# Side work put in front of a block until its tokens are there, and one function table for ScalarE

## The chip, the cores and the metric

The kernel runs on one core of a Trainium2 chip. Its engines each run their own instructions in the order in which the program wrote them, and wait for each other by semaphores: PE (TensorE, matmuls), DVE (VectorE), ACT (ScalarE), POOL (GpSimd) and SP (SyncE, which here only issues DMAs). The metric is device time in microseconds (us) for one launch; smaller is better.

## What is computed

7168 tokens of 192 numbers pass three stages: a causal convolution over 7 tokens whose weights are a softmax of their own for each token and head, then a mixture of 8 experts of which each token takes its best two, then a second mixture of which each token takes one.

```python
w = softmax(weight_gen)                                # attention: 7 taps, 8 heads
out = einsum('bshk,bskhg->bshg', w, windows_of(x))
# first mixture, top 2 of noisy logits
noisy = x @ w_gate + log1p(exp(x @ w_noise)) * noise
for e in range(8):                                     # tokens whose top 2 hold e
    out[mask] += top2_w * (relu(x[mask] @ w1[e]) @ w2[e])   # 192 -> 1024 -> 192
# second mixture, top 1 of softmax(x @ w_gate)
for e in range(8):
    out[mask] = gate * (relu(x[mask] @ w1[e]) @ w2[e])
```

## The kernel before

The work has **five phases**. Phases 0, 1 and 2 are the first mixture, each for a group of tokens; phases 3 and 4 are the second. Within a phase the tokens are sorted by expert into blocks of 128, and one or two blocks of an expert make a **unit**. A phase can begin once it is routed: the logits of its tokens, the choice of experts, and the lists `src` (which token stands where) and `dest` (where its result goes) are there.

A unit runs as follows. POOL gathers each block's token rows with an indirect DMA (`gt<-rows,src`, `load_x`), SP transposes them by DMA (`xt<-gt`, `turn_x`), PE multiplies with the first weights (L1, `ph<-xt,wres`; numbers in fp32 are carried as pairs of fp16, so that 5 matmuls make 128 of the 1024 hidden values), ACT makes the high half of the rectified result (`hh<-ph`) and DVE the low half (`hl<-ph,hh`), PE multiplies with the second weights (L2, `py<-wres,hh` and `py<-wres,hl`), ACT copies the sum out (`yo<-py`, two buffers), and POOL scatters it (`ybuf<-yo,dest` in phases 0 to 2, `out_dram<-yo,dest` later). A unit of one block has two L1 steps of 20 matmuls (128x128) and 24 L2 matmuls, a unit of two blocks four steps of 10 (128x256) and 48.

The main loop over units writes the L1 steps of unit i alternating with the L2 steps of unit i-1 (`l1_step` at 1487, `l1_late`, `l2_step`, loop at the end of the kernel). Gathers are issued up to three units ahead (`prepare`), but only of phases that are routed. Where the next unit belongs to a phase that isn't routed yet, the loop first writes all L2 steps of the last unit and then everything that the routing still needs (`feed.until(lambda: ph.ready)`), and only then the gathers and the L1 of that unit.

Everything else is **side work**: the convolution and its taps (`acc`, `tmp`, `xs`, `wg`), splitting the experts' weights into fp16 halves (`wres`, `wacc`, `wsc`, `wbt`; small matmuls `pm<-wacc,onesf` add up a scale), logits, the routing of the next phase (`lg`, `ra`, `rb`, `rc`, `rd`; `pr<-msk,..`, `pr<-bex,pex`, `pr<-rb,lost`, then `src`, `segt`, `ge`, `pr<-ge,ones`, `be`, `dest`), and combining results. It is written as threads of steps, and a planner decides at build time where each step stands. The planner (`Clock`, 77) keeps a modelled time for every engine and buffer from fixed costs. `Feed.pump` (257) is called after each L1 step and each L2 step: it takes steps, as long as there are any whose inputs the model has ready by the time at which PE is free (`clk.free["P"]`), with a small allowance for each engine, and writes them there. `clk.ready(a)` is the modelled time at which a buffer is written. On the chip nothing of that model remains; only the order does.

All recorded instructions of the helper carry its line, L189, so rows are told apart by names. ACT's functions come in tables, and the compiler writes a table load (ACT_TABLE_LOAD) in front of a function whose table isn't the loaded one. Exp, Ln, Relu, Abs, Copy and Square are used.

Of the kernel before, what the change touches and what calls it, by code (L numbers as in the profile page):

```python
# [16 lines left out]
P = 128  # L17
# [193 lines left out]
class Feed:  # L211
# [42 lines left out]
                best = (t + th[2], th)  # L254
        return best and best[1]

    def pump(self):
        while True:
            th = self.pick(self.clk.free["P"])
            if th is None:  # L260
                return
            self.step(th)
# [9 lines left out]
def moe_kernel(ctx: ExitStack, tc: tile.TileContext, x: bass.AP, wgen: bass.AP,  # L272
               g1: bass.AP, n1: bass.AP, noise: bass.AP, w11: bass.AP, w12: bass.AP,
               g2: bass.AP, w21: bass.AP, w22: bass.AP, out: bass.AP):
    nc = tc.nc
    clk = Clock()
    V, A, G, PE, SP = [Eng(e, k, clk) for e, k in (
        (nc.vector, "V"), (nc.scalar, "A"), (nc.gpsimd, "G"), (nc.tensor, "P"), (nc.sync, "S"))]
    feed = Feed(clk)

    def new_pool(name, side=None, **kw):
        if side:
            kw["side"] = side
        return Pool(tc.alloc_tile_pool(name=name, bufs=1, **kw), clk, name.startswith("ps"))
# [1063 lines left out]
    for pi, ph in enumerate(phases):  # L1348
# [6 lines left out]
        for it in dyn + [None] + stat if pi == 2 else stat + dyn + [None]:  # L1355
# [4 lines left out]
            u = Unit()  # L1360
# [126 lines left out]
    def l1_step(u, s):  # L1487
        T = u.nb * P
        fs = 512 // T
        ps = psm.tile([P, 512], F32, name="ph", bufs=4)  # L1490
        for fi in range(fs):
            f = s * fs + fi
            w = u.w1[f // 4]
            fo = (f % 4) * P
            o = ps[:, fi * T:(fi + 1) * T]
            for j, (wo, xi) in enumerate(((0, 0), (0, 2), (512, 0), (1024, 1), (1024, 3))):
                PE.matmul(o, w[:, wo + fo:wo + fo + P], u.xt[:, xi], start=(j == 0), stop=(j == 4))
        hh = blk.tile([P, 512], F16, name="hh", bufs=5)
        hl = blk.tile([P, 2 * RW], F16, name="hl", bufs=5)[:, 0:512]
        A.activation(hh, ps, AF.Relu)  # L1500
        u.h.append((hh, hl))
        late.append((ps, hh, hl))
# [98 lines left out]
    def seldom(ph):  # L1601
# [7 lines left out]
        with tc.If(used > ph.ndyn):  # L1609
            with tc.For_i(b0, used + ph.base, NR) as i:  # L1610
                us = []
                for k in range(NR):
                    u = Unit()
                    u.ph, u.nb, u.b0, u.e, u.rare, u.last = ph, 1, 0, None, True, False
                    u.ns, u.h = 2, []
                    u.src, u.dest, u.bei = [blk.tile([P, 1], I32, name=f"{v}{k}") for v in ("srcr", "destr", "beir")]
                    V.tensor_copy(u.src, ph.src[:, ds(i + k, 1)])
                    V.tensor_copy(u.dest, ph.dest[:, ds(i + k, 1)])
                    V.tensor_copy(u.bei, ph.bei[:, ds(i + (k - ph.base), 1)])
                    us.append(u)  # L1620
                for u in us:
                    load_x(u)
                for k, u in enumerate(us):
                    turn_x(u)
                    if ph.m:
                        u.gate = blk.tile([P, 1], F32, name=f"gater{k}")
                        V.tensor_tensor(u.gate, u.g[0][:, 256:257], ph.undo[:, ds(i + (k - ph.base), 1)], op=ALU.mult)
                for u in us:
                    for half, step in enumerate((l1_step, l2_step)):
                        for _ in fetch(u, half):  # L1630
                            pass
                        for k in range(u.ns):
                            step(u, k)
                            l1_late()
                    l2_out(u)
# [38 lines left out]
    for i in range(nu + 1):  # L1674
        u = units[i] if i < nu else None
# [35 lines left out]
        for k in range(n):  # L1711
            while s1 < n1 and s1 * n <= k * n1:
                l1_step(u, s1)
                s1 += 1
                if s1 == n1 and u.last:
                    passed.add((u.e, 0))
                    feed.n += 1
                feed.pump()
            l1_late()
            for _ in range(4 // n):  # L1720
                next(jobs, None)
            if TP:
                turns(i)
            while s2 < n2 and (s2 + 1) * n <= (k + 1) * n2:
                l2_step(prev, s2)
                s2 += 1
                if s2 == n2:
                    l2_out(prev)
                feed.pump()
# [39 lines left out]
```

## Time and profile before

| | before |
|---|---|
| median of 3 runs | 1016.14 us (1012.07 to 1022.45) |
| the profiled execution | 1023.41 us, its span 1021.6 us |
| mean granted TensorE clock in it | 0.945 of full speed |
| PE busy | 899.0 us, 88% of the span |
| DVE busy | 761.2 us, 75% |
| ACT busy | 511.9 us, 50% |
| POOL busy | 431.4 us, 42% |

A row of the timeline gives start, length, engine, line, operation, what is written from what, the tile, and in brackets how long the engine was idle just before and what ended that. Starts are us from the span's start. The granted clock is a share of full speed: 1.00 stands for 2.4 GHz, 0.50 for 1.2 GHz. SPq and POOLq are an engine's sequencer, which issues DMAs.

### The profile page before, as it was taken

To read this page: it belongs to the slowest core of one execution; us is meant where nothing else is said; L and a number is where in the kernel's file an instruction comes from. 1 tells how busy PE (TensorE), PEld (TensorE's weight loads), DVE (VectorE), ACT (ScalarE), POOL (GpSimd) and SP (SyncE) were. 2 spreads that over 40 slices of the span, in tenths; PEclk is the share of its full clock that TensorE was granted. 3 is DMA by queue.
4 is the path that set the end of the run, shared out by engine and by line. 5 is a ranking of instruction groups with operands and counts; after the bars stand their busy time and mean duration, and the time that the engine had idled before them with its cause. 6 is when DMAs were issued, how large, how long until landed. Compare 5 with 4: busy or idle time off the path is not lost. (4 is left out here: it accounts for less than half of the span.)

```text
span 1021.6 us, 26687 instructions
## 1 busy us (share of the span) xinstructions
PE 899.0 (88%) x10354; PEld 828.4 (81%) x10354; DVE 761.2 (75%) x1854; ACT 511.9 (50%) x1024; POOL 431.4 (42%) x575
## 2 busy tenths in 40 slices
PE   2896269999997999999679999999989998999985
PEld 0453158989996799999679988998989998999985
DVE  7587758999987798968577768988678987355442
ACT  1333147774441444546356778855666633444432
POOL 4020035555534455543443434444545443464541
PEclk8898569999998899999789999999999999999998
DMA  9257079998671678653489999856468547453692
GB/s 278 58 135 159 0 139 226 244 201 188 155 144 41 158 162 175 166 116 112 112 178 260 205 205 251 191 129 155 115 175 191 126 118 210 98 121 85 196 241 81
DMA packets 216802, 160.97 MB, mean 158 GB/s; under 512 B 147996, under 2 KB 198511, under 8 KB 216668
## 3 DMA queue, kind: packets, MB, share of 16 engines
q1 hardware_dynamic: 197932, 114.34, 46.7%
q0 software_dynamic: 18736, 44.85, 18.8%
q8 instruction: 84, 1.38, 0.6%
q14 instruction: 50, 0.41, 0.1%
HBM read 74.46 MB, written 32.59 MB: 105 GB/s over the span
## 5 line engine op out<-in xcount | busy, mean ns | idle before, releaser
L189 ACT ACTIVATE hh<-ph 128x512 f16<-128x512 f32 x362 | 214.8, 595 | 325.8 <-PE ph L189 284.3
L189 PE MATMUL ph<-xt,wres 128*128 128x256 f16 (+1 forms) x3200 | 327.1, 255 | 24.7 <-DMA xt<-gt 13.1
L189 DVE SCALAR_TENSOR_TENSOR hl<-ph,hh 128x512 f16<-128x512 f32 x362 | 245.5, 685 | 114.5 <-ACT hh L189 101.2
L189 PEld LDWEIGHTS <-wres 128*128 128x128 f16 x3200 | 265.0, 100 | 46.8 <-issue 20.3
L189 PE MATMUL py<-wres,hh 128*128 128x192 f16 x2048 | 273.9, 247 | 7.0 <-ACT yo L189 6.4
L189 PEld LDWEIGHTS <-hh 128*128 128x128 f16 x2896 | 261.0, 98 | 14.1 <-issue 9.4
L189 POOL DMA_INDIRECT gt<-rows,src x181 | 195.8, 1082 | 144.4 <-DVE wmx L189 72.6
L189 POOL DMA_INDIRECT ybuf<-yo,dest x120 | 138.5, 1154 | 271.8 <-ACT yo L189 258.6
L189 PE MATMUL py<-wres,hl 128*128 128x192 f16 x1024 | 253.0, 247 | 0.0
L189 PE MATMUL ph<-xt,w 128*128 128x128 f16 (+1 forms) x1600 | 136.8, 240 | 18.6 <-DMA xt<-gt 7.6
L189 PEld LDWEIGHTS <-hl 128*128 128x128 f16 x1448 | 142.0, 98 | 0.3 <-DVE hl L189 0.2
L189 PEld LDWEIGHTS <-w 128*128 128x128 f16 x1600 | 115.8, 100 | 26.9 <-issue 8.9
L189 POOL DMA_INDIRECT out_dram<-yo,dest x61 | 63.4, 1039 | 120.7 <-ACT yo L189 70.4
L189 PE MATMUL py<-w,hh 128*128 128x192 f16 x848 | 114.0, 248 | 0.1
L189 PE MATMUL py<-w,hl 128*128 128x192 f16 x424 | 105.0, 248 | 0.0
L189 PE MATMUL acc<-prod,identf 128*128 128x384 f32 x168 | 63.1, 535 | 14.1 <-DVE prod L189 11.7
L189 PEld LDWEIGHTS acc<-prod,identf 128*128 128x128 f32 x168 | 34.1, 208 | 36.5 <-DVE prod L189 11.7
L189 DVE COPY w<-wres 128x3072 f16 x53 | 51.0, 968 | 13.2 <-issue 5.8
L189 ACT ACTIVATE yo<-py 128x192 f32<-128x192 f32 x120 | 37.1, 327 | 38.5 <-DMA ybuf<-yo,dest 22.8
L189 DVE SCALAR_TENSOR_TENSOR wres<-w,wsc,wres 128x1024 f16<-128x1024 f32 (+1 forms) x32 | 49.4, 1545 | 4.9 <-ACT wres L189 4.9
L189 ACT ACTIVATE wres<-w,wsc 128x1024 f16<-128x1024 f32 (+1 forms) x32 | 43.5, 1359 | 12.2 <-DVE wsc L189 11.4
L189 DVE TENSOR_TENSOR acc<-acc,tmp 128x768 f32<-128x768 f32 (+1 forms) x60 | 47.9, 798 | 2.1
(206 smaller groups left out, 901.3 us busy)
## 6 DMA issues: line engine op xcount, KB each, us to landing
w<-wres SPq DMA_DIRECT2D x23, 768.0 KB
rows<-rows SPq DMA_DIRECT2D x24, 512.0 KB
w<-in_moe_w_dram SPq DMA_DIRECT2D x14, 768.0 KB
w<-in_moe_w_dram SPq DMA_DIRECT2D x13, 512.0 KB
xs<-in_x_dram SPq DMA_DIRECT2D x6, 960.0 KB
rows<-ybuf SPq DMA_DIRECT2D x10, 384.0 KB
yl<-ybuf SPq DMA_DIRECT2D x10, 384.0 KB
wres<-wbt SPq DMA_DIRECT2D x56, 64.0 KB
```

The source lines that it names most:

```text
L189: return fn(*args, **kw)
```

## The change

Three edits. `pump` may be given a time up to which side steps are taken in, later than PE's modelled free time. Before the first L1 step of each unit that isn't a rarely run one, `pump` is called with the later of the modelled times at which the unit's transposed tokens and its first weights are there; steps that can start by then are written ahead of the unit's matmuls. And one call at the kernel's start loads a table that holds both Exp and Ln.

```diff
-    def pump(self):
+    def pump(self, upto=0.0):
         while True:
-            th = self.pick(self.clk.free["P"])
+            th = self.pick(max(upto, self.clk.free["P"]))
             if th is None:
                 return
             self.step(th)
...
     feed = Feed(clk)
+    nc.scalar.preload_act_table_set("natural_log_exp_and_others")
...
     def l1_step(u, s):
         T = u.nb * P
         fs = 512 // T
+        if s == 0 and not u.rare:
+            feed.pump(max(clk.ready(a) for a in (u.xt, u.w1[0])))
         ps = psm.tile([P, 512], F32, name="ph", bufs=4)
```

The order on ACT around the first block, before. The first rc is the end of the first part of phase 0's noise, `ra` and the second `rc` belong to its second part, and the first `hh` is that of the first block:

```order
L189 ACT_TABLE_LOAD
L189 ACTIVATE rc<-rb 128x128
L189 ACTIVATE ra<-lg_128 128x64
L189 ACT_TABLE_LOAD
L189 ACTIVATE ra<-ra 128x64
L189 ACT_TABLE_LOAD
L189 ACTIVATE rc<-rb 128x64
L189 ACTIVATE hh<-ph 128x512
L189 ACT_TABLE_LOAD
L189 ACTIVATE wg_541<-wg_541 128x112
L189 ACTIVATE wres,wacc_930<-w_352 128x1536
```

The same stretch of ACT in the change:

```order
L189 ACTIVATE rc<-rb 128x128
L189 ACTIVATE ra<-lg_129 128x64
L189 ACTIVATE ra<-ra 128x64
L189 ACTIVATE rc<-rb 128x64
L189 ACTIVATE wg_542<-wg_542 128x112
L189 ACTIVATE wres,wacc_918<-w_353 128x1536
L189 ACTIVATE wres<-w_353,wsc_922 128x2x512
L189 ACTIVATE wbt_927<-w_353,wsc_922 128x512
L189 ACTIVATE hh<-ph 128x512
```

The table loads are gone, and a softmax of the convolution (`wg`) and three weight passes stand ahead of the first block's `hh`. On PE, likewise, `pr<-identf,ra` and a `pm<-wacc,onesf` now stand ahead of the first block's first matmul; in before they stood behind its first 20 and first 50.

The order on POOL at the end of phase 0, before. The first row is the scatter of a block of the unit two before the last; `spacer` is a short memset; each gather is of phase 1:

```order
L189 DMA ybuf_68<-yo,dest 9216x192
L189 MEMSET spacer 1x1
L189 DMA ybuf_68<-yo,dest 9216x192
L189 MEMSET spacer 1x1
L189 DMA ybuf_68<-yo,dest 9216x192
L189 MEMSET spacer 1x1
L189 DMA ybuf_68<-yo,dest 9216x192
L189 DMA gt<-rows_66,src 128x256 x10
L189 MEMSET spacer 1x1
```

The same place of POOL in the change, from the same scatter on:

```order
L189 DMA ybuf_69<-yo,dest 9216x192
L189 DMA gt<-rows_67,src 128x256 x6
L189 MEMSET spacer 1x1
L189 DMA ybuf_69<-yo,dest 9216x192
L189 MEMSET spacer 1x1
L189 DMA ybuf_69<-yo,dest 9216x192
L189 DMA gt<-rows_67,src 128x256 x2
L189 MEMSET spacer 1x1
L189 DMA ybuf_69<-yo,dest 9216x192
```

Six gathers of phase 1 moved ahead of the last three scatters of phase 0, and the others alternate with scatters.

The order on DVE where phase 1's list of tokens is done, before. `ISA src` is the last row that the gathers need; no `hl` (a block's low half) stands here:

```order
L189 ISA src<-rb,rc 128x176
L189 TENSOR_TENSOR segt<-segs,id_95 128x16
L189 TENSOR_REDUCE segt<-segt 128x1
L189 TENSOR_SCALAR ge<-ip,segt 16x56
L189 CAST be<-pr 128x56
L189 TENSOR_SCALAR be<-be 128x56
L189 CAST be<-segs 128x1
L189 TENSOR_SCALAR rd<-ra 128x88
```

The same place of DVE in the change:

```order
L189 ISA src<-rb,rc 128x176
L189 TENSOR_TENSOR segt<-segs,id_96 128x16
L189 TENSOR_REDUCE segt<-segt 128x1
L189 TENSOR_SCALAR ge<-ip,segt 16x56
L189 SCALAR_TENSOR_TENSOR hl<-ph,hh 128x512
L189 TENSOR_TENSOR tmp<-xs_3469,wg_3470 128x768
L189 TENSOR_TENSOR acc_4091<-acc_4091,tmp 128x768
L189 SCALAR_TENSOR_TENSOR hl<-ph,hh 128x512
L189 CAST be<-pr 128x56
```

Two `hl` of blocks still stand behind `src`: phase 1's routing is done while blocks of phase 0 run. On PE, `pr<-rb,lost` moved forward by the same way: in before it stands right ahead of phase 1's first matmul, in the change ahead of the last unit's L1.

## Rows read from the trace of the kernel before

**Rows 1.** The page, busy us (share of the span) x instructions of each engine.

```profile
PE 899.0 (88%) x10354; PEld 828.4 (81%) x10354; DVE 761.2 (75%) x1854; ACT 511.9 (50%) x1024; POOL 431.4 (42%) x575
```

**Rows 2.** Windows: stretch, length, busy by engine, granted clock, DMA share, GB/s.

```profile
100.00:150.00 50.00, 19.17 (x160) 16.13 (x159) 32.34 (x110) 10.83 (x16) 8.66 (x10) 0.55 0.27 58
150.00:200.00 50.00, 47.36 (x514) 44.22 (x512) 44.26 (x97) 40.00 (x67) 26.25 (x29) 1.00 1.02 228
...
300.00:350.00 50.00, 39.97 (x399) 35.95 (x397) 38.06 (x111) 13.97 (x26) 17.91 (x22) 0.86 0.35 82
```

**Rows 3.** Waits of PE: who waited for what, us in total, times, longest.

```profile
PE ph L189 <- DMA xt<-gt: 20.7, 4, 10.0
...
PE ph L189 <- issue: 9.5, 1, 9.5
...
PE pm L189 <- ACT wres L189: 1.6, 2, 0.8
```

**Rows 4.** Timeline of PE at the first block.

```profile
140.04 2.29 PE L189 MATMUL ph<-xt,wres 128*128 128x128 f16 x20 [9.50 <-issue]
142.26 0.65 PE L189 MATMUL pr<-identf,ra 128*39 128x128 f32 x2
...
146.43 0.28 PE L189 MATMUL pm<-wacc,onesf 128*128 128x1 f32 x2
```

**Rows 5.** Groups of ACT by line: busy us, mean ns, idle before.

```profile
L189 ACT ACT_TABLE_LOAD x11 | 14.1, 1283 | 3.0 <-DMA wres<-in_weight_gen_dram 2.8
```

**Rows 6.** Timeline of ACT in the routing of phase 0.

```profile
95.38 1.28 ACT L189 ACT_TABLE_LOAD   x1
96.67 0.31 ACT L189 ACTIVATE rc<-rb 128x128 f32<-128x128 f32 x1
...
104.89 1.28 ACT L189 ACT_TABLE_LOAD   x1
```

**Rows 7.** Timeline of DVE in the same stretch.

```profile
97.01 0.29 DVE L189 SCALAR_TENSOR_TENSOR rb<-rb,ra 128x128 f32<-128x128 f32 x1 [1.85 <-ACT rc L189]
...
104.90 0.19 DVE L189 TENSOR_SCALAR rb<-ra 128x64 f32<-128x64 f32 x1 [1.89 <-ACT ra L189]
```

**Rows 8.** Timeline of PE, phase 0 to phase 1.

```profile
312.92 1.28 PE L189 MATMUL ph<-xt,wres 128*128 128x128 f16 x20
314.04 0.33 PE L189 MATMUL py<-wres,hh 128*128 128x192 f16 x2
314.20 0.25 PE L189 MATMUL py<-wres,hl 128*128 128x192 f16 x1
...
323.94 0.45 PE L189 MATMUL pr<-rb,lost 39*128 39x88 f32 x2
334.43 2.29 PE L189 MATMUL ph<-xt,wres 128*128 128x256 f16 x10 [10.03 <-DMA xt<-gt]
```

**Rows 9.** Timeline of DVE at the same place.

```profile
325.87 0.21 DVE L189 TENSOR_SCALAR src<-ra 128x88 int32<-128x88 f32 x1
```

**Rows 10.** Timeline of POOL at the same place.

```profile
314.51 0.99 POOL L189 DMA_INDIRECT ybuf<-yo,dest  x1 [0.22 <-issue]
...
326.99 0.98 POOL L189 DMA_INDIRECT gt<-rows,src  x1 [1.10 <-DVE segt L189]
```

**Rows 11.** Windows behind two gaps, columns as in rows 2.

```profile
334.40:340.00 5.60, 5.58 (x27) 3.72 (x28) 2.95 (x10) 2.69 (x4) 2.74 (x3) 0.50 0.87 168
...
524.40:527.80 3.40, 3.40 (x30) 3.30 (x28) 3.16 (x9) 2.64 (x6) 2.01 (x3) 0.50 1.06 83
```

**Rows 12.** Timeline of PE and POOL, phase 1 to phase 2 and after.

```profile
505.68 4.42 PE L189 MATMUL ph<-xt,w 128*128 128x128 f16 x40 [7.58 <-DMA xt<-gt]
...
523.23 1.32 PE L189 MATMUL ph<-xt,w 128*128 128x128 f16 x20 [2.74 <-DVE w L189]
...
496.59 1.00 POOL L189 DMA_INDIRECT ybuf<-yo,dest  x1 [4.18 <-ACT yo L189]
497.89 0.98 POOL L189 DMA_INDIRECT gt<-rows,src  x1 [0.30 <-issue]
```

## Prediction

> **What bounds the kernel now.** I read the page's first part first: TensorE (PE) is busy 899.0 of 1021.6 us, VectorE (DVE) 75% [rows 1]. A PE at 88% leaves 122 us of gaps and of matmuls at a lower clock, so I looked for these with the table of windows. Two of the three stretches shown in [rows 2] are poor: 100 to 150 us (PE 19.17 of 50, granted clock 0.55) and 300 to 350 us (39.97, clock 0.86); at 150 to 200 us PE has 47.36 of 50 at clock 1.00. The list of waits says what PE waits for there: 9.5 us once for "issue" (the first block) and 20.7 us in four waits for the transposed tokens xt, the longest 10.0 [rows 3]. The timeline puts places to them: the first block's L1 starts at 140.04 after 9.50 us idle [rows 4]; the first block of phase 1 starts at 334.43 after 10.03 us idle [rows 8]; the first of phase 2 at 505.68 after 7.58 us [rows 12]. These are the places where a block's tokens come late, and so those where this change can act. Inside a phase PE runs without a gap and a moved step changes only the order.
>
> Each such gap costs more than itself. Behind the gap at 334 us the granted clock is 0.50 (the 1.2 GHz level) from 334.4 to 340.0 [rows 11]: 5.6 us at half speed, 2.8 us lost. Behind a gap of 2.74 us at 523.23 [rows 12] it is 0.50 for 3.4 us [rows 11]: 1.7 us lost.
>
> **Part one, the table of functions.** Before has 11 table loads of 1283 ns on ScalarE (ACT), 14.1 us together [rows 5]; the order of the change has one, ahead of everything. What a load is worth depends on who waits. Over the span ACT is half idle [rows 1], so I count the loads among the blocks at nothing: what hides them is that PE runs other matmuls until hh comes, and where that cover fails up to 1.28 us more is won for each. Three loads lie in the chain that routes phase 0, before any block can run, the first at 95.38, the last at 104.89 [rows 6]. DVE has nothing else to do then: it sits 1.85 us until rc comes at 97.01, 1.89 us until ra at 104.90 [rows 7], and again until the Ln behind the third load. Without them the chain is shorter by at most 3 x 1.283 = 3.85 us. The third load starts at 104.89 and rb takes 0.19 us of DVE from 104.90 beside it, which stays, and the logits that DVE scales after the first chain have their own time from PE; I take 3.5 us, with 2.6 (two loads) and 3.85 as ends.
>
> The row shows the Ln of the first load starting at 96.67, which is 1.29 us after the load began [rows 6]: the load costs its own length and nothing behind it. The Trainium skill, page "ScalarE: Activation LUTs", section "What ACT_TABLE_LOAD costs", states about 1283 ns for the load, as here, and about 1380 ns more for a drain, 2.66 us for each switch; by that page the three would be worth about 8 us, an estimate, and the forecast about 4.5 us lower. No run here shows that drain after a load; one that lies ahead of the load would be hidden in the idle of ACT, so I go by the rows.
>
> **Part two, the first block.** The new call stands ahead of the first matmuls of each unit. At the very first one it puts the steps that can start by then into the 9.50 us wait. On PE two rows move in front: pr<-identf,ra, 0.65 us, and pm<-wacc, 0.28 us, which in before stood behind the first 20 matmuls and more [rows 4]. That is 0.9 us less behind the wait, at the half clock too. On ACT the softmax of the conv weights and the first expert's weight passes move ahead of the first hh. On DVE conv taps and a weight pass move ahead of the first hl. If they run over the 9.50 us, PE waits for hl at its first L2: between nothing and 0.8 us, the longest wait of PE for a weight pass in before [rows 3]. So this part lies between -0.9 and -0.1; I take -0.1, since both DVE and ACT get more to do ahead of that L2, and with the table loads **the start gives -3.6 us**.
>
> **Part three, the boundary from phase 0 to phase 1.** This is the large term. In before the routing of phase 1 ends behind the last block of phase 0. PE's lost counts (pr<-rb,lost) run at 323.94, DVE writes the list src at 325.87, POOL issues the first gather at 326.99 [rows 8 to 10], and PE's next matmul is the block at 334.43 [rows 8]. From gather to L1 is 7.44 us (gather, transpose, landing). The last unit's L2 has been drained by then, since the program waits here when the phase isn't routed. All engines but POOL and SP idle.
>
> In the order of the change the routing of phase 1 stands earlier against the blocks: six gathers stand on POOL ahead of three scatters that preceded them before, and on DVE the src row has an hl of phase 0 in front and two more right behind. The first new gather follows the scatter that in before started at 314.51 and took 0.99 us [rows 10]. I set that scatter as mark: in before the unit it belongs to ended its matmuls at 312.92, where the next x20 begins [rows 8]. So with E = 312.92 the scatter ends at E + 2.6 and the gather starts at E + 2.9 (0.30 us between POOL's rows [rows 12]). src is ready by then, as its rows stand ahead of the last unit. L1 of phase 1 then comes at E + 2.9 + 7.44 = E + 10.3. What can PE do between? By the order: two L1 steps of the last unit (x20 at 1.12 us from start to start each [rows 8]), 24 and 24 matmuls of L2 at 0.08 us (two in 0.16 [rows 8]), and a few small ones of routing and gates, which I put at 0.5 to 1.0 us beside the 0.45 of the lost counts: 2.2 + 3.9 + 0.5 to 1.0 = 6.7 to 7.2 us. A gap of 3.1 to 3.6 us is left, of the size of that at 523 us, and so with 1.7 us of half clock: 5.3 us at most, against 10.03 + 2.8 = 12.8 us before. The last unit's L2 is now emitted between L1 steps of phase 1, not drained, so it fills nothing in that gap but isn't lost either. **Boundary: -7.5 us**. Ends: -5 (the transposes land two to three us later, because they now share DMA with the traffic of blocks; at the boundary to phase 2 their wait is 7.58 us) and -12.8 (whole gap hidden).
>
> What a wait more costs here: the six gathers stand on POOL in order, so the scatters behind them come up to 6 x 1.3 us later (0.98 and 0.30 for each). yo has two buffers, so ACT's copies of the last unit, and then PE's py, wait for the scatters. I leave it inside the lower end.
>
> **Part four, the rest.** The boundary to phase 2 at 505.68 is bound on POOL: the first gather at 497.89 follows a scatter at 496.59 directly, not DVE [rows 12]. The change moves the routing of phase 2 some two us later against the blocks; I count 0, and 2 us slower where DVE takes POOL's place as the last. Inside phases only orders change: 0, with 2 us either way.
>
> **Sum.** 1023.41 is the profiled run (its span 1021.6 us and 1.8 around it). -3.6 - 7.5 = -11.1 us gives 1012.3. The median of before, 1016.14, lies 7.3 us (0.7%) under this run, which is within what three runs scatter (1012.07 to 1022.45). Against the median the forecast is 1016.1 - 11.1 = **1005 us**, a ratio of 0.989. About 1% (10 us) is what a measurement of this kernel can tell from no change.
>
> **Rivals.** (a) The forecast, 0.45: 1002 to 1008.
> (b) The gap at phase 1 closes altogether and PE's clock stays at its upper level: -12.8 - 3.6 = -16.4, **1000 us**. For it: the routing stands early enough; POOL's gather need only come 3 us sooner. Against it: the scatter of the unit before stands in front of the gather. 0.2.
> (c) The start is won and the boundary hardly: transposes queue behind the DMA traffic of blocks (DMA share 1.02 at 150 to 200 us [rows 2]), or the 7.58 us gap at phase 2 grows by what phase 1 starts earlier. -3.6 and 0 to -3: **1011 us**, 0.25.
> (d) Slower. The call puts matmuls of side work in front of a block's own on a queue that runs in order, if the planner's clock says that their inputs are there first. If its clock is wrong, PE stands for them. This phase has 16 weight pieces with one small matmul each, which waits for ACT's pass over a piece. In before the worst such waits are 0.8 us (pm behind ACT wres) [rows 3] and 2.74 us (ph behind DVE's copy w) [rows 12], each rarely. Sixteen at 0.8 us make 12.8, more than the 11.1 won; it decides from 0.7 us each. At the 2.74 us row it would be 44 - 11 = 33 us slower. At 1.4 us each: 22 - 11 = +11, **1027 us**. For it: DVE has 44.26 of 50 busy and DMA 1.02 in that phase [rows 2], so the inputs do run late at times. Against it: a step goes ahead only where the modelled input is ready, and in before the same planner left no such wait above 0.8 us. 0.1. The Trainium skill, "TensorE: Matmul & The Clock Gate", section "Step-by-step: what each phase is for", speaks for this rival: matmuls stay in program order and only weight loads are pulled ahead; nothing in the rows above shows a matmul overtaking.
>
> **How the numbers follow.** The range reaches from (b), 1000 less 2 us for the rest and 1 for the table loads' upper end, to (c) with the rest at +2 to 3: **997 to 1014**; outside lie (d) and a tenth of the others. Faster by over 1% means 1006.0 or less: two thirds of (a), all of (b), little of (c): 0.52. Within 1%: the rest of (a) and (c): 0.39. Slower: most of (d), 0.09.
>
> **What would show it.** Right: one table load; the first L1 at 136 to 137 us of the span; the first gather of phase 1 directly behind the scatter of the unit before, with phase 0's last L2 still to come, and the gap ahead of its L1 at 2 to 5 us, with clock 0.50 behind it for some 3 us. Wrong: a gap there of over 7 us (c) or none (b); waits of pm or pr for ACT, DVE or DMA that add up to over 10 us in 140 to 330 us (d); DVE's hl waits ahead of the first L2; the gap ahead of phase 2 grown by more than 2 us.

## The result and the profile after

The changed kernel takes 1004.43 us (median of 14 runs, 999.61 to 1013.91) against 1018.45 us of the kernel before (14 runs beside them, 1012.07 to 1022.45): ratio **0.9872**, 95% interval 0.9848 to 0.9897, that is 14.0 us or 1.3% faster. The forecast was 1005 us, a ratio of 0.989, faster by 11.1 us. Its range held the time. Later sets of runs did not agree on the gain: in one where the kernel before takes 1065 us the whole change gave nothing, in one where it takes 1021 us it gave 18.4 us, and in one at 1057 us, which had the parts alone, these gave little. That is the subject of most of the experiments.

The page after, and PE's list of waits:

```profile
PE 893.2 (89%) x10354; PEld 826.2 (83%) x10354; DVE 763.3 (76%) x1853; ACT 500.3 (50%) x1015; POOL 429.0 (43%) x575
...
PE ph L189 <- DMA xt<-gt: 15.4, 4, 7.1
...
PE pm L189 <- ACT wres L189: 7.0, 5, 3.1
...
PE py L189 <- ACT yo L189: 1.3, 4, 0.4
```

PE is busy for 893.2 us where it was 899.0 [rows 1], with the same 10354 matmuls, at a mean granted clock of 0.955 where it was 0.945. Its longest wait for tokens is 7.1 us instead of 10.0 [rows 3]. The wait of `pm` for a weight pass on ACT grew from 1.6 to 7.0 us, of which 3.1 lie ahead of the first block, where PE has nothing else to do. The line for "issue" (9.5 us at the first block) is gone, because other rows of PE now stand in that wait. The wait is divided by them and hardly filled: 1.86, 3.14 and 3.51 us of it are left, as the rows of PE below show.

**The chain ahead of the first block**, on ACT, DVE and POOL of the changed kernel, to be held against [rows 6] and [rows 7]:

```profile
93.86 0.41 ACT L189 ACTIVATE rows<-rows 128x256 f16<-128x256 f16 x1 [0.64 <-DVE rows L189]
94.18 0.29 ACT L189 ACTIVATE rc<-rb 128x128 f32<-128x128 f32 x1
...
100.85 0.26 ACT L189 ACTIVATE ra<-lg 128x64 f32<-128x64 f32 x1 [6.38 <-DVE lg L189]
101.14 0.26 ACT L189 ACTIVATE ra<-ra 128x64 f32<-128x64 f32 x1
101.65 0.26 ACT L189 ACTIVATE rc<-rb 128x64 f32<-128x64 f32 x1 [0.26 <-DVE rb L189]
```

```profile
94.50 0.29 DVE L189 SCALAR_TENSOR_TENSOR rb<-rb,ra 128x128 f32<-128x128 f32 x1 [0.43 <-ACT rc L189]
...
101.43 0.19 DVE L189 TENSOR_SCALAR rb<-ra 128x64 f32<-128x64 f32 x1 [0.61 <-ACT ra L189]
101.94 0.23 DVE L189 SCALAR_TENSOR_TENSOR rb<-rb,ra 128x64 f32<-128x64 f32 x1 [0.32 <-ACT rc L189]
```

```profile
129.58 1.09 POOL L189 DMA_INDIRECT gt<-rows,src  x1 [69.17 <-DVE wmx L189]
```

The same two ends of the chain in before:

```profile
94.94 0.42 ACT L189 ACTIVATE rows<-rows 128x256 f16<-128x256 f16 x1 [0.64 <-DVE rows L189]
...
134.13 1.02 POOL L189 DMA_INDIRECT gt<-rows,src  x1 [72.63 <-DVE wmx L189]
```

Nothing stands between `rows` and `rc` any more, and DVE's waits of 1.85 and 1.89 us shrank to 0.43 and 0.61. From the start of the last `rows<-rows` ahead of the chain to the first gather it is 129.58 - 93.86 = 35.72 us. In before it is 134.13 - 94.94 = 39.19 us. The difference is 3.47 us. The rest of the earlier start, 1.08 us, was there before the chain began and differs between any two executions.

**The first block and the boundary to phase 1**, PE and POOL:

```profile
127.85 0.65 PE L189 MATMUL pr<-identf,ra 128*39 128x128 f32 x2 [1.86 <-DVE ra L189]
131.63 0.59 PE L189 MATMUL pm<-wacc,onesf 128*128 128x1 f32 x2 [3.14 <-ACT wres L189]
135.73 6.11 PE L189 MATMUL ph<-xt,wres 128*128 128x128 f16 x50 [3.51 <-DMA xt<-gt]
...
148.29 0.38 PE L189 MATMUL pm<-wacc,onesf 128*128 128x1 f32 x2 [1.73 <-ACT wres L189]
...
310.48 1.28 PE L189 MATMUL ph<-xt,wres 128*128 128x128 f16 x20
...
314.06 1.28 PE L189 MATMUL ph<-xt,wres 128*128 128x128 f16 x20
...
320.96 3.35 PE L189 MATMUL ph<-xt,wres 128*128 128x256 f16 x20 [3.64 <-DMA xt<-gt]
```

```profile
312.12 1.01 POOL L189 DMA_INDIRECT ybuf<-yo,dest  x1 [0.22 <-issue]
313.44 0.98 POOL L189 DMA_INDIRECT gt<-rows,src  x1 [0.30 <-DVE acc L189]
```

```profile
320.96:324.00 3.04, 3.04 (x20) 2.39 (x21) 2.94 (x4) 0.60 (x1) 2.61 (x5) 0.69 1.22 124
324.00:327.00 3.00, 3.00 (x26) 2.74 (x25) 2.90 (x4) 0.60 (x1) 2.69 (x2) 0.75 0.72 153
327.00:330.00 3.00, 3.00 (x33) 2.79 (x31) 2.96 (x5) 1.53 (x3) 1.25 (x4) 1.00 0.29 87
```

The windows have the columns of [rows 2]. PE starts phase 1 after a gap of 3.64 us, where it was 10.03 [rows 8]. The first gather stands directly behind the scatter, as the order had it, 0.30 us after its end, and 7.52 us ahead of the L1. Behind the gap the clock is 0.69 and 0.75 in two windows of 3 us and then 1.00: (0.31 x 3.04) + (0.25 x 3.00) = 1.7 us lost.

### The profile page after: what moved, and what is told of

It reads as the page before. It is cut to its first block, busy times and chain, and to the rows that moved or that the text cites. A ratio compares the mean times of both kernels' runs of the same rounds, so it can differ in the third digit from the quotient of the medians.

```text
span 999.2 us, 26672 instructions
## 1 busy us (share of the span) xinstructions
PE 893.2 (89%) x10354; PEld 826.2 (83%) x10354; DVE 763.3 (76%) x1853; ACT 500.3 (50%) x1015; POOL 429.0 (43%) x575
## 5 line engine op out<-in xcount | busy, mean ns | idle before, releaser
L189 POOL DMA_INDIRECT gt<-rows,src x181 | 199.1, 1100 | 136.3 <-DVE wmx L189 69.2
L189 POOL DMA_INDIRECT ybuf<-yo,dest x120 | 133.7, 1115 | 263.0 <-ACT yo L189 241.2
```

Source lines behind the costliest of these rows:

```text
L189: return fn(*args, **kw)
```

## Experiments

Each was run beside the kernel before in the same set, and its ratio is to that; e6 and e12 are single runs, made for their traces. The record names the chip of each of these sets: number 3 for e1 to e8, where the kernel before takes 1057 and 1065 us, and number 7 for e9 to e12, where it takes 1021 us. For the first set it names none.

### The two parts apart: e1 and e2

e1 keeps only the table load, e2 only the call.

```diff
 e1:
-        if s == 0 and not u.rare:
+        if s == 0 and False:
 e2:
-    nc.scalar.preload_act_table_set("natural_log_exp_and_others")
```

> The table of functions loaded once, and nothing else of the change: the new call ahead of a unit's first L1 step is left out. By the forecast only the three loads in the chain that routes phase 0 count: 3.5 us less, ratio 0.9966, the first gather about 3.5 us earlier against the first rc of that chain (beginning of rc to first gather 37.5 us in before, 35.4 after the change with one load ahead of the rc gone too), the gap ahead of phase 1 at 10 us as in before. By the rule of 2.66 us for each switch some 8 us would come off before the first gather, ratio 0.992. If the loads inside the phases delay PE as well, up to 14 us, ratio 0.986.

> The call ahead of a unit's first L1 step alone, with the 11 table loads of before. By the forecast the boundary to phase 1 gives 7.5 us and the start next to nothing: 1011 against 1018.45, ratio 0.992 to 0.993, gap ahead of phase 1 at 3 to 4 us. If the later phases gain from the order too, as the two traces seem to say (some 7 us between 511 and 839 us), ratio 0.986 or less. If the two parts need each other, ratio over 0.996.

The kernel before took 1057.4 us in this set. e1 gave a ratio of 0.9974 (0.9944 to 1.0004), within its interval the forecast's 0.9966 and neither 0.992 nor 0.986. Its gap ahead of phase 1 is 10.33 us, as expected. e2 gave **1.0064** (1.0038 to 1.0090): the call alone made the kernel slower here, against every expectation of a gain. So either the boundary's gain wasn't one, or something in this set took it back.

### The call by phases: e3 and e4

e3 calls `pump` only for units of phase 0, e4 only for those of the later phases; both keep the table.

```diff
 e3:
-        if s == 0 and not u.rare:
+        if s == 0 and not u.rare and u.pi == 0:
 e4:
+        if s == 0 and not u.rare and u.pi >= 1:
```

> The table and the call, but the call only for units of phase 0. By the forecast this is the whole of the change: 1004 to 1007, ratio 0.987 to 0.989, gap ahead of phase 1 at 3 to 4 us. If the later phases gain by the call (rival), ratio 0.992 to 0.995, since some 7 us are missing.

> The table and the call, but the call only for units of phases 1 to 4. By the forecast this gives the table's 3.5 us and no more: ratio 0.9965, with 2 us either way, gap ahead of phase 1 at 10 us as in before. If the later phases gain by the call (rival), ratio 0.988 to 0.992.

e3 gave 0.9971 (0.9939 to 1.0004), e4 0.9936 (0.9910 to 0.9962), in the same set as e1 and e2. Neither tells the theories apart: the call that should win all wins nothing over the table alone (e1, 0.9974), and the one that should win nothing wins some. In e4 the gap ahead of phase 1 is 7.09 us, too, and not the 10 us expected.

### Again, with the kernel before traced beside it: e5 to e8

In e3 the gathers of phase 1 started early, as in the changed kernel (322.30 us), but PE's first L1 of that phase came 11.75 us behind the first one instead of 7.5. The next set therefore held the whole change (e5), the kernel before (e6, for its trace), a version that puts the gathers ahead of the scatters (e7), and e3 again (e8).

```diff
 e7, at the end of a unit's L2:
                 if s2 == n2:
+                    nxt = todo["load"]
+                    if u is not None and nxt < nu and nxt > i and units[nxt].pi != u.pi and units[nxt].ph.ready:
+                        prepare(min(i + 1, nxt), False)
                     l2_out(prev)
```

> The whole change once more. In the four runs so far (the kernel before at 1057 us there) the boundary's gain showed only in part: between the first gathers of phase 1 and its first L1, PE got its instructions one or two at a time, about 0.7 us apart, though it waited for nothing that the trace shows. Theory 1: that is where these runs were made, and not the change; then the whole change gives 0.9872 again where the kernel before takes about 1018 us, and 0.995 to 1.0 where it takes 1057 us, with the same stall of 5 to 8 us ahead of phase 1. Theory 2: the earlier result was a lucky order; then the ratio is over 0.993 anywhere.

> The kernel before, for its trace beside the others of this set. Theory 1: where the set runs at 1057 us, the share of PE's idle time that nothing visible ends is as large here as in the changed kernels, but in the 10 us wait ahead of phase 1 it costs nothing; where the set runs at 1018 us there is next to none of it. Theory 2: there is none of it in the kernel before in either case.

> The whole change, and one thing more: when the next gathers are the first of a new phase that is routed, they are issued ahead of the scatters of the unit before and not behind them. After the change the first gather of phase 1 starts 0.3 us behind a scatter at 312.12, and its list was ready 2.8 us before. If that scatter is what bounds the gather (the step on which the forecast's 3.1 to 3.6 us of remaining gap rest), the gap of 3.64 us falls to about 1 us, the clock stays at its upper level there, and the kernel is 3 to 5 us faster than the whole change. If the transposes or the list bound it, the gap stays, and the time with it.

> The table and the call for units of phase 0 only, once more, beside the whole change. By the forecast it gives all of the change's gain within 2 us. If the order in phases 1 to 4 gives the 3 us that the result lies under the sum (14 against 11), it is 3 us or more behind the whole change.

The kernel before took 1065.38 us here. e5 gave 1.0020 (0.9990 to 1.0051), e7 1.0007 (0.9979 to 1.0034), e8 0.9935 (0.9907 to 0.9963). So the whole change is worth nothing in this set; theory 1 had 0.995 to 1.0 for such a set. e8 was expected within 2 us of e5, or 3 us and more behind it. It did neither: its ratio is 0.0085 below that of e5, some 9 us, and the two intervals don't meet. In this set the call in the later phases costs time. PE at the end of phase 0 in e5 (its L1 rows):

```profile
322.58 0.61 PE L189 MATMUL ph<-xt,wres 128*128 128x128 f16 x8
323.68 0.27 PE L189 MATMUL ph<-xt,wres 128*128 128x128 f16 x2 [0.49 <-issue]
324.41 0.22 PE L189 MATMUL ph<-xt,wres 128*128 128x128 f16 x1 [0.46 <-issue]
325.12 0.28 PE L189 MATMUL ph<-xt,wres 128*128 128x128 f16 x2 [0.50 <-issue]
...
327.97 0.28 PE L189 MATMUL ph<-xt,wres 128*128 128x128 f16 x2 [0.49 <-issue]
...
334.06 2.13 PE L189 MATMUL ph<-xt,wres 128*128 128x256 f16 x14
```

The first gather of phase 1 in e5 and the row of ACT behind that step:

```profile
321.95 0.98 POOL L189 DMA_INDIRECT gt<-rows,src  x1 [0.30 <-issue]
...
331.19 0.60 ACT L189 ACTIVATE hh<-ph 128x512 f16<-128x512 f32 x1 [9.86 <-remote]
```

One L1 step of 20 matmuls, which took 1.28 us in before [rows 8], is spread over 5.7 us: one to three matmuls every 0.71 us, and no row shows what they wait for. It begins about 1.1 us behind the start of the first gather (321.95) and goes on until 331, past the end of the sixth (329.2). In after the same step (314.06, 1.28 us) runs beside the same six gathers, from 313.44 on, without a gap. ACT's row on that step starts at 331.19 after 9.86 us of idle time, 2.9 us behind the step's last matmul, and DVE waits for ACT. So PE is the one that is late at this boundary, and not the tokens: the L1 of phase 1 at 334.06 follows PE's own work without a gap, 12.1 us behind the first gather. In e6 it is the old picture:

```profile
340.26 2.08 PE L189 MATMUL ph<-xt,wres 128*128 128x256 f16 x9 [10.02 <-DMA xt<-gt]
```

From the first L1 to that of phase 1 e6 takes 340.26 - 138.17 = 202.1 us and e5 334.06 - 134.64 = 199.4. The boundary's 7.5 us are 2.7 here. The chain of the table loads is shorter by 3.46 us in this pair too (35.73 against 39.19 us). More is lost in phase 2: from its first L1 to the first scatter into the output e6 takes 766.83 - 515.38 = 251.5 us and e5 767.40 - 510.61 = 256.8. But e7, with the same call there, takes 253.0 and e8, without it, 254.0, so this stretch differs by some us from trace to trace, and these traces don't show what the loss belongs to.

Both kernels of this set have short stalls of PE without a visible cause (0.2 to 1.0 us each, ahead of a weight load of PE and behind 140 us): 33 us in 71 stalls in e6 and 42 us in 88 in e5, against 7.3 us in 19 and 5.0 us in 11 in the traces of before and after that the forecast was held against. In e5, 51 of the 88 begin 1.0 to 2.5 us behind the start of a gather, a time that makes up 27% of the stretch. (The traces of this set hold some 11,300 to 11,800 semaphore events where those of before and after hold 17,000, so a part of them may be waits whose end isn't shown. But counted whatever ended them, the idle pieces of that length ahead of a weight load make 41 us in e6 and 52 in e5, against 12 and 11, so the difference is there.) The transfers of the program's code don't account for it: the pages of e5 and e10 have the same 84 packets at 0.6% of the time in that queue (q8), and none of them runs in e5 between 322 and 331 us. This answers the second theory on e6: the stalls are in the kernel before too, and in its 10 us wait ahead of phase 1 there is nothing to stall.

e7 was to show whether the scatter bounds the first gather. It doesn't show it: its first gather comes 2.9 us earlier against PE's work (at the last unit's first L1 step), but PE is fed in the same slow way from 327 to 337 us, and the time is that of e5. Whether it would win where PE isn't held up stays untried.

### A third set: e9 to e12

e9 is e1 again, e10 the whole change. e11 limits the gathers ahead of a new phase's first L1 to those of its first unit. e12 gathers 32 bytes more for each token, into a buffer that nobody reads, so its time includes work that the reference doesn't need.

```diff
 e11, in prepare:
+            if units[todo["load"]].pi != units[i].pi and todo["load"] > i + 1:
+                break
             load_x(units[todo["load"]])
 e12, in load_x:
+            if not u.rare:
+                tiny = blk.tile([P, 8], F32, name="tiny", bufs=6)
+                G.indirect_dma_start(out=tiny, out_offset=None, in_=noise[:, :],
+                                     in_offset=bass.IndirectOffsetOnAxis(
+                                         ap=u.ph.src[:, u.b0 + sb:u.b0 + sb + 1], axis=0),
+                                     bounds_check=N - 1, oob_is_err=False)
```

> The table loaded once and nothing else, once more. By the trace of the change the loads bring the first gather 3.47 us forward and count nowhere else: ratio 0.9966 to 0.9974, as in the first set (0.9974), whatever the kernel before takes here.

> The whole change a third time. Theory 1 (the stalls of PE without a visible cause belong to the place where the set runs, and eat what the earlier gathers win): ratio 0.985 to 0.990 where the kernel before takes about 1018 us and the trace has under 20 short stalls of that kind after 140 us; 0.997 to 1.004 where it takes 1057 us or more and has over 60. Theory 2 (the first result was chance): over 0.993 in both.

> The whole change, but ahead of phase 1's first L1 only the two gathers that its first unit needs, and not six; the others follow behind the next scatters. If it is the run of six gathers that feeds PE one or two instructions at a time for 7 us there (slow place), the stall shrinks to some 2 us at this point and the first L1 of phase 1 comes 10 us behind the first gather at most instead of 12.1; the other gathers then stall PE behind it, so that the time changes by less than 3 us. If the stall belongs to the place in the program (PE's instructions there) or to the transposes, it stays at 6 to 7 us. At a fast place the time stays that of the whole change within 3 us.

> The whole change, and behind each gather of a block a second one with the same list that fetches 32 bytes for each token from another table into a buffer that nobody reads: 181 gathers more, each of 128 rows, with hardly any bytes. If it is the gather as such that stalls PE (slow place: 51 of 88 short stalls of PE begin 1.0 to 2.5 us behind a gather's start, which is 27% of the time), the short stalls grow from 42 us by half or more, and the time by over 20 us. If it is the bytes, or something else at that time, they stay within 10 us, and the time grows by what POOL's longer run puts ahead of the phases' first blocks, under 15 us. At a fast place: under 10 us of such stalls in either case.

The kernel before took 1020.87 us in this set. **e10 gave 0.9816** (0.9780 to 0.9852), 18.4 us faster, and its trace has 10 short stalls of PE with 4.2 us in all. Theory 1's numbers for such a set were 0.985 to 0.990, which only the end of the interval reaches; theory 2 (chance) asked for over 0.993. e9 gave 0.9947 (0.9919 to 0.9974): the forecast's 0.9966 is inside, and so, just, is the 0.992 of 2.66 us for each load, which the chain below decides. The call is worth 1015.89 - 1002.43 = 13.5 us beside the table here. PE at the boundary in e9 and in e10:

```profile
328.11 2.29 PE L189 MATMUL ph<-xt,wres 128*128 128x256 f16 x10 [10.23 <-DMA xt<-gt]
```

```profile
322.02 1.23 PE L189 MATMUL ph<-xt,wres 128*128 128x256 f16 x9 [4.32 <-DMA xt<-gt]
```

e11 gave 0.9950 (0.9920 to 0.9980), 11.9 us slower than e10. That is outside its 3 us. The gap ahead of phase 1 is 3.29 us, so six gathers or two make no difference there. But the limit holds at every change of phase. Two waits of PE that e10 doesn't have at these places, one for a copy of ACT and one for tokens:

```profile
342.24 0.48 PE L189 MATMUL py<-wres,hh 128*128 128x192 f16 x2 [2.82 <-ACT yo L189]
...
861.94 2.31 PE L189 MATMUL ph<-xt,wres 128*128 128x128 f16 x20 [4.05 <-DMA xt<-gt]
```

They are 6.9 us together; where the rest of the 11.9 us goes isn't shown.

For the stall it tells nothing, since this set has hardly any. The same holds for e12: 8.6 us of short stalls, under the 10 expected for such a set, so the question of gathers or bytes stays open. Its 1037.64 us (one run) are 35 us over e10, more than the 15 expected. POOL issues the gathers of phase 1 only from 329.88 on, behind two scatters more of phase 0 than in e10, and the gap ahead of phase 1 is 10.50 us again:

```profile
338.55 3.70 PE L189 MATMUL ph<-xt,wres 128*128 128x256 f16 x20 [10.50 <-DMA xt<-gt]
```

## Why the prediction was right

Two pairs of traces without the slow feeding of PE tell where the time went: before and after, and e9 (the table alone) and e10 (the whole change). The stretches lie between rows of the same work.

| stretch, us | before | e9 | after | e10 | mean of after - before and e10 - e9 |
|---|---|---|---|---|---|
| first L1 to first L1 of phase 1 | 194.39 | 194.21 | 185.23 | 188.39 | -7.5 |
| from there to the first L1 of phase 2 | 171.25 | 169.59 | 170.13 | 170.55 | -0.1 |
| from there to the first scatter into the output | 232.97 | 231.93 | 228.46 | 226.70 | -4.9 |
| from there to the end | 282.95 | 278.67 | 279.65 | 280.73 | -0.6 |

The two differences are -9.2 and -5.8, -1.1 and +1.0, -4.5 and -5.2, -3.3 and +2.1. The first of each also holds the table loads among the blocks. These are single traces: the spans of the pairs differ by 22.4 and 8.3 us where the medians differ by 14.0 and 13.5, so a stretch is uncertain by some us, and only what both pairs share is read.

**The table loads: right to a tenth of a microsecond.** I took 3.5 us; the chain from `rows` to the first gather is 39.2 us with them (before, e2, e6) and 35.7 to 35.9 without (all other runs): 3.3 to 3.5 us, whether the kernel before takes 1018 or 1065 us. Between 3.85 - 0.19 and 2.6 no row gave 3.5, so the last tenth is luck. The loads elsewhere I counted at nothing; phase 0 bears that out (194.21 us in e9 against 194.39), and in the later stretches the two differ by 1 to 4 us, which one pair can't put down to the loads. The 2.66 us for each switch that the Trainium skill states (page "ScalarE: Activation LUTs", section "What ACT_TABLE_LOAD costs") would have made it about 8 us, an estimate from that page; here three loads were worth 3.47 us in the first pair, 1.16 each. The prediction left open a drain ahead of a load, in ACT's idle time. The rows show none: the last `rows<-rows` of before ends at 94.94 + 0.42 = 95.36, the load stands at 95.38 to 96.66, and `rc` starts at 96.67 [rows 6].

**The start.** The rows moved ahead of the first L1 cost nothing there. The first L2 didn't wait for hl; instead PE waited 1.73 us for a weight pass at 148.29, since ACT stood 2.96 us for the weights' DMA with a block's hh behind it:

```profile
146.66 1.48 ACT L189 ACTIVATE wres<-w 128x1536 f16<-128x1536 f32 x1 [2.96 <-DMA w<-in_moe_w_dram]
```

So the kind of loss was right and its size about double the 0.8 us, which also makes it the small edition of rival (d). Behind the first L1 PE's waits for such passes went from 1.6 to 3.9 us, and those for yo, which the prediction feared to grow, from 6.4 to 1.3. In before:

```profile
PE py L189 <- ACT yo L189: 6.4, 6, 1.7
```

**The boundary.** Forecast: the gather 0.3 us behind the scatter, 10.3 us from the unit's end to L1, a gap of 3.1 to 3.6 us and 1.7 us of lower clock, -7.5 us in all. Measured in after: 0.30, 320.96 - 310.48 = 10.5 us, a gap of 3.64 us (4.32 in e10), 1.7 us, and -7.5 us in the mean of the pairs (-9.2 and -5.8; that their mean meets the forecast exactly is luck). The gather, the gap and the clock came as the prediction had them. A part of that stretch is 24 matmuls of L2 (2 us) that now run behind the L1; the next stretch takes them in and is still not longer in the mean. The earlier return of the clock would fit that (1.7 us lost instead of 2.8), but the two pairs differ in sign there. Rival (b), no gap at all, fell: the scatter did stand in front. Rival (c) fell where PE was fed without stalls.

**The rest: sized too small.** I counted the later phases at 0 with 2 us either way, for the reason that PE runs without a gap inside a phase. Phase 2 isn't like that: in e9 PE is idle for 7.4 of the first 39 us behind its start. The boundary to phase 2 did stay (7.58 before, 7.14 after), but phase 2 itself became 4.9 us shorter. Windows of phase 2 up to the first scatter into the output, e9 and then e10:

```profile
497.70:537.00 39.30, 31.92 (x351) 29.51 (x352) 24.90 (x58) 20.08 (x48) 13.38 (x18) 0.82 0.76 165
537.00:729.63 192.63, 188.03 (x2358) 178.93 (x2356) 155.33 (x463) 135.18 (x259) 87.02 (x117) 1.00 0.80 190
```

```profile
492.57:531.90 39.33, 32.62 (x403) 30.72 (x404) 29.03 (x71) 23.25 (x54) 12.88 (x17) 0.90 0.75 188
531.90:719.27 187.37, 184.34 (x2307) 175.85 (x2305) 150.35 (x449) 133.52 (x254) 84.11 (x117) 1.00 0.84 190
```

With the same number of matmuls (2709 and 2710) PE is idle for 12.0 us in e9 and 9.7 in e10, and busy for 220.0 and 217.0: in the first 39 us it does 52 matmuls more at a clock of 0.90 instead of 0.82. So matmuls that ran later now run in the stretch of short gaps behind the boundary to phase 2. That this is by the call in the units there is what the order suggests; e4, which has the call only in later phases, gained 0.4% beside the table alone (0.9936 and 0.9974), but in a set with stalls and with overlapping intervals, and e8, which lacks that call, beat e5. So it isn't shown.

**What the forecast did not have.** Where PE is fed slowly while a run of gathers is on, the tokens' arrival isn't the last thing at the boundary, and with the gathers the stall comes into PE's work too (e5). In before (e6) the gathers run in the wait, where PE has nothing that could be held up. No rival said so. (c) has the boundary nearly right in e5 (2.7 us won), with another cause, but it left 3.6 us and more of gain, and e5 has none. So that the forecast's time was met is in part the luck of the set: its sum was read from a trace with few stalls, its ratio of 0.989 lies far outside e5's 0.9990 to 1.0051, and in e10's set the gain is 18.4 us and not 11.1. Why a set has these stalls, and whether it is the gathers or their bytes, stays open. They stand with chip 3 and not with chip 7; no run here tells the chip from the time at which a set was run.

## What to carry to other kernels

A wait that everybody sits out is also cover: before filling it, ask what else runs badly in that time and is free only because nobody works. Price a removed table load by its own row (here 1.28 us, with nothing ahead of it or behind it) and only where the next engine waits for it, and count a gap on PE with the lower clock behind it (here 3.64 us of gap and 1.7 us more). And hold a change of one per cent against the kernel before in more than one set of runs, with a trace of it from each: here the same pair gave 0.987, 1.002 and 0.982.

## What the runs showed that I had not expected

PE can be held to one to three matmuls every 0.71 us for some 7 us with nothing in the trace that it waits for, while six gathers are issued (e5, 323 to 331 us; e2, e3, e7 and e8 at the same place in the program). In the set with before at 1021 us, 181 additional gathers of 32 bytes a token left such stalls at 8.6 us. The kernel before itself took 1018, 1057, 1065 and 1021 us in the four sets.
